# Filler matmuls that end with the first FFN tile, a wider planned pipe, and the first batch's mixing ahead

## Chip, cores and metric

The kernel runs on one core of a Trainium2 chip. The metric is the device time of one execution in microseconds. Before the change the median of three runs is 1138.97 us (1134.53 to 1140.03 us).

## What is computed

The inputs are q, k and v of 8 batches, 8 heads, 576 positions and 64 columns a head, all float32, and two FFN weights.

1. Attention with a mask. Heads 0 to 3 see the last 32 positions, heads 4 to 7 every fourth of the last 128. Scores are scaled by 1/8; softmax; product with v.
2. The heads are laid side by side: x of 8 batches, 576 rows, 512 columns.
3. Mixing: `u = x + real(fft(fft(x, axis=rows), axis=columns))`, then `un`, which is u with mean 0 and variance 1 per row.
4. FFN: `u + relu(un @ w_ch1) @ w_ch2`, hidden width 2048.

## The kernel before, in words

Every instruction is added to a plan (class `Plan`) with its engine, a cost in us, the buffers that it reads and writes, and a priority, lower first. `Plan.run` is a list scheduler: it plays the operations through with these costs, gives each free engine the ready operation with the lowest priority, and so fixes the order of the instructions on each engine, TensorE, VectorE, ScalarE, POOL and SP's DMA queue among them. Only the order goes to the chip; there every engine keeps it and waits where data is late. Planned times are used for nothing else, so an operation that carries an earliest time (`at`) doesn't wait for it on the chip.

The plan knows one pipe for all transfers: each takes the pipe for its bytes divided by 2.7e5 (bytes per us, line 322) and is done 1.6 us later. At most eight transfers of an issuing engine are open at a time. Buffers of a kind form a ring: a buffer is placed in the order of creation, and only when the one that had its slot is finished with.

The work has two halves. In the first, three kinds run side by side on TensorE:

- attention: per batch twelve steps, each with score matmuls (line 546), the mask with a minimum on VectorE (555), the exponential on ScalarE (561), transposes (574) and their copy (577), the product with v (581) and the scaling (593). Step u of batch b has priority 12b + u. A batch needs four loads each of `tq`, `kb` and `vt`; there are two `tq`, three `kb` and four `vt` buffers. Results go to DRAM (628) with priority plus `P_ST`, or `P_ST0` for batch 0.
- mixing, per batch: loads (700, 709), folds on POOL and VectorE (712 to 736), matmuls with cosine and sine tables along rows (763, 785) and columns (809, 815), sums on POOL (677, 679), normalisation (642 to 656). Its priority is 12(b + 1) + `P_MIX` + `P_SPAN` * x with x from 0 to 1; batches 0 and 1 have `P_MIX0`, `P_SPAN0` and `P_MIX1`, `P_SPAN1`. Its loads add `P_FD`, for batch 0 `P_FD0`. The tables `seq`, `tail`, `chn` and `alt` are loaded through POOL's queue with `at` from `T_SEQ` and `T_CHN`.
- the early FFN: the first 6 of 16 hidden blocks for each pair of 128-row tiles. `fill` writes up matmuls (943), a ReLU split in a high and a low part (949, 951), and down matmuls (959). It has priority `P_FILL` + `P_FILLT` * tile, 45 and up. The up results and the sums of the down matmuls take turns on two PSUM banks, the ring `ff`.

Weights come as float64 and are converted and split on the chip: `prep_w(f, ...)`, for f from 0 to 5, loads two blocks of 512 KB (881) into stage buffers of the ring `ut` (four slots) and runs one ScalarE, four VectorE, one ScalarE and one POOL operation on each (882 to 901); the POOL operation in line 901 is the last and is called the split below. The priority is `P_W` + `P_WF` * f, that of the load is `P_WD` lower. The same ring `ut` gives the operand buffer of each early-FFN pair (669, 670), created after the twelve stages.

In the second half, from the last line-959 matmul on, the other ten hidden blocks are done by lines 1204 and 1240 for all rows in nine equal chunks.

The zero fillers (line 492) are matmuls on a tile of zeros whose result nobody reads. There are `NSPIN` = 150 groups of two, with priority 900, so the plan puts one in wherever TensorE would have nothing else to do, group n from 0.4n us on. Their target is one tile of the ring `ff`, the first that is created.

Of the kernel before, what the change touches and what calls it, by code (L numbers as in the profile page):

```python
# [32 lines left out]
NH = 8  # L33
NXB = 6
NLATE = 4
NSPIN = 150
NPE = 1
LO1 = 'DVE'
NFA = 5
P_QK0, P_V0 = -8.0, -7.0  # L40
P_ST, P_FD, P_WD, P_ST0, P_FD0, P_SPAN0, P_SPAN1 = -4.0, -12.0, -10.0, 0.0, 0.0, 8.0, 13.0
P_QK, P_V, P_TR, P_MIX, P_SPAN, P_W, P_WF, P_FILL, P_FILLT = -8.0, -7.0, -5.0, 2.0, 13.0, 8.0, 8.0, 45.0, 4.0
P_MIX0, P_MIX1 = 3.0, 0.0
T_SEQ, T_CHN = 16.0, 24.0
NCH = B * S // TOK
NREST = 4 * B
QB = 96
# [132 lines left out]
class Plan:  # L180
# [21 lines left out]
    def add(self, eng, cost, fn, r=(), w=(), prio=0.0, nbytes=0, at=0.0):  # L202
        op = Op()
        op.eng, op.cost, op.fn, op.prio, op.nbytes = eng, cost, fn, prio, nbytes
        op.num, op.after, op.ready, op.start = len(self.ops), [], at, None
        self.ops.append(op)
        deps, bufs = set(), {}
        for items, writes in ((r, False), (w, True)):
            for it in items:
                b, key = it if isinstance(it, tuple) else (it, None)  # L210
                bufs[id(b)] = b
                keys = set(b.writer) | set(b.readers) if key is None else {key, None}
                for x in keys:
                    if x in b.writer:
                        deps.add(b.writer[x])
                    if writes:
                        deps.update(b.readers.get(x, ()))
        for items, writes in ((r, False), (w, True)):
            for it in items:
                b, key = it if isinstance(it, tuple) else (it, None)  # L220
                if writes:
                    if key is None:
                        b.writer, b.readers = {None: op.num}, {}
                    else:
                        b.writer[key] = op.num
                        b.readers.pop(key, None)
                else:
                    b.readers.setdefault(key, []).append(op.num)
        op.bufs = list(bufs.values())
        for b in op.bufs:  # L230
            b.left += 1
        deps.discard(op.num)
        op.waits = len(deps)
        for d in deps:
            self.ops[d].after.append(op)
        return op

    def run(self):
        ops = self.ops
        busy = {}  # L240
        avail, soon = {}, {}
        turn = {t: 0 for t in self.tags}
        events = [0.0]
        dma = 0.0
        for o in ops:
            busy.setdefault(o.eng, 0.0)
            avail.setdefault(o.eng, [])
            soon.setdefault(o.eng, [])
            if not o.waits:
                heapq.heappush(soon[o.eng], (o.ready, o.num))  # L250
                heapq.heappush(events, o.ready)
        order = []
        used, clock = {}, [0, False]
        lanes = {e: [] for e in busy}

        def place(o, now):
            need = []
            if o.nbytes and len(lanes[o.eng]) >= 8 and lanes[o.eng][-8] > now:
                return False
            for b in o.bufs:  # L260
                if b.tag is None or b.ap is not None or b.free_at is not None:
                    continue
                line, k = self.tags[b.tag], turn[b.tag]
                if line[k] is not b:
                    return False
                if k == 0 and any(x.left or x.free_at > now for t in self.behind.get(b.tag, ()) for x in self.tags.get(t, ())):
                    return False
                if k >= self.slots[b.tag]:
                    old = line[k - self.slots[b.tag]]
                    if old.left or old.free_at > now:  # L270
                        return False
                need.append(b)
            for b in need:
                turn[b.tag] += 1
                b.free_at = -1.0
            return True

        while events:
            now = heapq.heappop(events)
            while events and events[0] <= now:  # L280
                heapq.heappop(events)
            again = True
            while again:
                again = False
                for eng in busy:
                    if busy[eng] > now:
                        continue
                    while soon[eng] and soon[eng][0][0] <= now:
                        _, n = heapq.heappop(soon[eng])
                        heapq.heappush(avail[eng], (ops[n].prio, n))  # L290
                    held, got = [], None
                    while avail[eng]:
                        e = heapq.heappop(avail[eng])
                        if place(ops[e[1]], now):
                            got = ops[e[1]]
                            break
                        held.append(e)
                        if len(held) > 60:
                            break
                    for e in held:  # L300
                        heapq.heappush(avail[eng], e)
                    if got is None:
                        continue
                    again = True
                    got.start = now
                    order.append(got)
                    cost = got.cost
                    if eng == "PE":
                        win = int(now / WINDOW)
                        while clock[0] < win:  # L310
                            load = used.get(clock[0], 0.0) / WINDOW
                            clock[1] = load > 0.45 if clock[1] else load > 0.75
                            clock[0] += 1
                        cost *= 1 if clock[1] else 2
                        used[win] = used.get(win, 0.0) + min(cost, (win + 1) * WINDOW - now)
                        used[win + 1] = used.get(win + 1, 0.0) + max(0.0, now + cost - (win + 1) * WINDOW)
                    end = now + cost
                    busy[eng] = end
                    heapq.heappush(events, end)
                    done = end  # L320
                    if got.nbytes:
                        dma = max(dma, end + 0.9) + got.nbytes / 2.7e5
                        done = dma + 1.6
                        lanes[eng].append(done)
                        heapq.heappush(events, done)
                    for a in got.after:
                        lag = self.OWN[eng] if a.eng == eng else self.LAG[eng]
                        a.ready = max(a.ready, done + lag)
                        a.waits -= 1
                        if not a.waits:  # L330
                            heapq.heappush(soon[a.eng], (a.ready, a.num))
                            heapq.heappush(events, a.ready)
                    for b in got.bufs:
                        b.left -= 1
                        b.free_at = max(b.free_at or 0.0, done + self.LAG[eng])
                        if not b.left:
                            heapq.heappush(events, b.free_at)
        if len(order) != len(ops):
            left = [o for o in ops if o.start is None]
            raise RuntimeError(f"{len(left)} operations can't be placed: {[(o.eng, o.num, o.prio) for o in left[:5]]}")  # L340
        self.length = max(busy.values())
        for o in order:
            o.fn()
# [20 lines left out]


SOON = -1.0
WINDOW = 4096 / 1200
PLAIN_MASK = (1, 0, 0, 0, 0, 0)
DIL_MASK = (1, 2, 0, 1, 2, 0)
# [3 lines left out]
def fused_kernel(ctx: ExitStack, tc, q, k, v, w1, w2, seq, tail, chn, alt, mask, ident, perm, flip, out):  # L373
    nc = tc.nc
    plan = Plan()
    add = plan.add
# [43 lines left out]
    def bank(tag):  # L420
        return ring(tag, views[tag])
# [53 lines left out]
    def start():  # L475
# [9 lines left out]
        for n, t in enumerate(kbs):  # L485
            zero(t, "DVE", 0.1, lambda t=t: nc.vector.memset(t()[:, 0:WIN], 0.0), "z", -6.0 + n)
        zero(blank, "DVE", 0.3, lambda: nc.vector.memset(blank().bitcast(F32), 0.0), None, -9.0)
        spin = bank("ff")
        for n in range(NSPIN):
            def turn_over():  # L490
                for _ in range(2):
                    nc.tensor.matmul(spin()[:, :2 * P], lhsT=blank()[:, :P], rhs=blank()[:, P:3 * P], start=True, stop=True)  # L492
            add("PE", 0.22, turn_over, (blank,), (spin,), 900.0, at=0.4 * n)
        for t in xs + xtail:
            zero(t, "DVE", 0.07, lambda t=t: nc.vector.memset(t()[:, C:C + 1], 0.0), "pad")
        def gaps():
# [825 lines left out]
```

## Time and profile before

| what | value |
|---|---|
| median of three runs | 1138.97 us |
| profiled execution, its own time | 1143.46 us |
| span in the profile | 1141.7 us |
| TensorE busy | 1097.8 us (96%) |
| VectorE busy | 737.1 us (65%) |
| ScalarE, POOL busy | 520.6 us (46%), 516.2 us (45%) |
| granted TensorE clock, mean | 0.987 |
| zero fillers, busy | 45.6 us in 300 matmuls, from 1.4 to 115.1 us |

The profile is that of one execution. Busy shares are means over stages with different limits, and matmuls of 492 count as busy like all others. PE is TensorE, DVE is VectorE, ACT is ScalarE, SPq is SyncE's DMA queue. PEclk 1.00 is 2.4 GHz; a value between 0.5 and 1 is a mix in time of 2.4 and 1.2 GHz.

### The profile page before, as it was taken

What the parts mean: (1) busy time and instruction counts of PE and PEld (TensorE: products, weight loads), DVE (VectorE), ACT (ScalarE), POOL (GpSimd) and SP (SyncE); (2) the same over time, 40 slices, a digit from 0 to 9 for tenths busy, and PEclk for the clock granted to TensorE, in tenths of its full rate; (3) what the DMA queues carried; (4) which work ended last, traced back from release to release, by engine and by line L of the source; (5) the groups of instructions that cost most, each with busy time, mean ns of one, the idle gap of its engine ahead of it and who ended that gap; (6) DMA issues with size and microseconds to landing.
All of it is one profiled execution on the core that took longest, in us unless ns stands there. A gap on an engine that the chain in (4) does not pass through costs nothing.

```text
span 1141.7 us, 21571 instructions
## 1 busy us (share of the span) xinstructions
PE 1097.8 (96%) x7750; PEld 976.1 (85%) x7750; DVE 737.1 (65%) x2177; ACT 520.6 (46%) x1282; POOL 516.2 (45%) x636
## 2 busy tenths in 40 slices
PE   9999999999999999999999999999999999999996
PEld 8887877897888888798988889898989898988885
DVE  6578978776576667877674437382837465555636
ACT  5566655465455353433442434334343434343432
POOL 2134553642253225463321466455564637372834
PEclk9998999999989999999999999999999999999998
DMA  9665646745373424344354303231415041423121
GB/s 329 182 219 174 193 133 182 216 144 168 113 207 95 141 75 132 130 139 134 103 161 102 120 1 80 78 93 57 110 39 139 19 130 38 111 58 91 56 75 38
DMA packets 103804, 137.14 MB, mean 120 GB/s; under 512 B 9144, under 2 KB 61816, under 8 KB 103696
## 3 DMA queue, kind: packets, MB, share of 16 engines
q1 hardware_dynamic: 100128, 126.85, 37.5%
q0 software_dynamic: 3040, 8.09, 2.4%
q8 instruction: 61, 1.00, 0.4%
q10 hardware_dynamic: 528, 0.82, 0.2%
q14 instruction: 47, 0.39, 0.1%
HBM read 97.92 MB, written 37.80 MB: 119 GB/s over the span
## 4 chain that ended last, share of the span: by engine, by line
PE 74%; DVE 13%; ACT 4%; issue 3%; POOL 2%; DMA 2%; SPq 0%; DVEq 0%; POOLq 0%; ACTq 0%
PE bank L1204 21%; PE bank L1240 17%; PE bank L943 10%; PE bank L959 9%; PE bank L581 4%; PE bank L546 4%; PE bank L809 2%; PE bank L574 2%; DVE low L901 2%; DVE pm L555 2%; PE bank L763 2%; PE bank L492 2%; ACT low L1083 2%; ACT pm L561 1%; DMA tq<-in_q_dram 1%
## 5 line engine op out<-in xcount | busy, mean ns | idle before, releaser
L1204 PE MATMUL bank<-low,wb 128*128 128x512 f32 x1080 | 264.9, 394 | 0.0
L1204 PEld LDWEIGHTS bank<-low,wb 128*128 128x128 f32 x1080 | 196.4, 188 | 41.8 <-POOL low L1086 3.5
L943 PE MATMUL bank<-ut,low 128*128 128x256 f32 x1296 | 176.5, 289 | 4.3 <-DVE low L951 3.2
L943 PEld LDWEIGHTS bank<-ut,low 128*128 128x128 f32 x1296 | 163.7, 193 | 8.0 <-DVE low L951 5.0
L561 ACT ACTIVATE pm<-pm,mx 96x128 f32<-96x128 f32 x384 | 131.5, 394 | 63.0 <-DVE mx L555 60.8
L1240 PEld LDWEIGHTS bank<-w2s,low 128*128 128x128 f32 x1134 | 144.9, 189 | 12.8 <-DVE low L901 6.7
L959 PE MATMUL bank<-low 128*128 128x512 f32 x648 | 155.0, 392 | 0.5 <-DVE low L951 0.5
L1240 PE MATMUL bank<-w2s,low 128*128 128x256 f32 x1134 | 150.1, 282 | 5.2 <-DVE low L901 4.7
L959 PEld LDWEIGHTS bank<-low 128*128 128x128 f32 x648 | 119.1, 188 | 24.1 <-DVE low L951 0.7
L901 DVE TENSOR_TENSOR low<-y,low 128x640 fp32r<-128x640 f32 x90 | 83.4, 927 | 86.3 <-ACT low L899 86.3
L899 ACT CAST low<-y 128x640 fp32r<-128x640 f32 x90 | 65.6, 729 | 153.1 <-POOL y L1226 118.8
L555 DVE CUSTOM_DVE_ANT_0 pm<-bank,mask_sb 96x128 f32<-96x128 f32 x384 | 92.6, 279 | 38.7 <-PE bank L546 37.1
L1222 POOL TENSOR_TENSOR y<-xa 128x256 f32<-128x256 f32 x45 | 33.3, 740 | 180.9 <-ACT xa L1210 180.8
L901 DVE TENSOR_TENSOR low<-xa,low 128x256 fp32r<-128x256 f32 x45 | 33.4, 743 | 119.6 <-ACT low L899 119.6
L1240 PE MATMUL bank<-low 128*128 128x256 f32 x756 | 98.7, 284 | 2.4 <-DVE low L901 2.3
L1240 PEld LDWEIGHTS bank<-low 128*128 128x128 f32 x756 | 94.7, 191 | 7.2 <-DVE low L901 5.0
L1210 ACT ACTIVATE xa<-bank 128x256 f32<-128x256 f32 x90 | 34.5, 384 | 129.4 <-PE bank L1204 128.3
L581 PE MATMUL bank<-vt,ptsb 128*96 128x65 f32 x768 | 85.7, 252 | 4.9 <-DVE xt L593 4.9
L581 PEld LDWEIGHTS bank<-vt,ptsb 128*96 128x96 f32 x768 | 78.0, 168 | 13.0 <-DVE xt L593 7.4
L951 DVE SCALAR_TENSOR_TENSOR low<-bank,low 128x256 fp32r<-128x256 f32 x108 | 45.3, 421 | 62.9 <-ACT low L949 62.2
L1033 DVE TENSOR_TENSOR ut<-ut,bank 128x512 f32<-128x512 f32 (+1 forms) x144 | 75.3, 548 | 4.6 <-PE bank L1240 1.3
L1066 DVE STREAM_TRANSPOSE ut<-ut 128x512 f32<-128x512 f32 (+1 forms) x76 | 70.8, 977 | 11.2 <-DMA ut<-us 11.1
(129 smaller groups left out, 1767.3 us busy)
## 6 DMA issues: line engine op xcount, KB each, us to landing
vt<-in_v_dram SPq DMA_DIRECT2D x32, 390.0 KB
wst<-in_w_dram SPq DMA_DIRECT2D x20, 512.0 KB
us<-uc SPq DMA_DIRECT2D x36, 257.0 KB
tq<-in_q_dram SPq DMA_DIRECT2D x32, 288.0 KB
part<-row SPq DMA_DIRECT2D x36, 256.0 KB
ut<-us SPq DMA_DIRECT2D x36, 256.0 KB
ut<-part SPq DMA_DIRECT2D x36, 256.0 KB
kb<-in_k_dram SPq DMA_DIRECT2D x31, 288.0 KB
```

Of the source, the lines that this page charges most:

```text
L546: nc.tensor.matmul(sc()[e][:QB, KB * n:KB * n + KB], lhsT=tq()[ps, QB * t:QB * t + QB], rhs=kb()[ps, QB * t:QB * t + KB], start=True, stop ...
L555: nc.vector.tensor_tensor_reduce(pm()[:, i], sc()[i % 2][:QB, KB * (i // 2):KB * (i // 2) + KB], mask_sb()[:, masks[blocks[i // 2]]], -0.1 ...
L561: add("ACT", 0.295, lambda i=i: nc.scalar.activation(out=pm()[:, i], in_=pm()[:, i], func=AF.Exp, bias=mx()[:, i:i + 1], scale=-1.0), ((mx ...
L581: add("PE", 0.16, lambda i=i: nc.tensor.matmul(av()[:QB, 65 * i:65 * i + 65], lhsT=pt()[:, i], rhs=vt()[:, i % 2, blocks[i // 2]], start=T ...
L899: add("ACT", act(n), lambda: nc.scalar.copy(out=dst(0), in_=src()), need, ((key[0], (key[1], 0)),), prio)
L901: add(eng, (pool if eng == "POOL" else dve)(n), lambda: lo.tensor_tensor(out=dst(1), in0=src(), in1=dst(0).bitcast(F32), op=ALU.subtract), ...
L943: nc.tensor.matmul(z()[:, :n_tok], lhsT=wf()[:, a, kk], rhs=ut()[:, p, kk], start=(kk == 0 and n == 0), stop=(kk == KT - 1 and n == 2),)
L959: nc.tensor.matmul(acc(), lhsT=h()[:, a, P * s:P * s + P], rhs=wf()[:, p], start=(first and n == 0), stop=(last and n == 2),)
L1033: add("DVE", dve(C if at in (outer, inner) else TOK1), lambda: nc.vector.tensor_tensor(out=blocks(part())[:, at], in0=blocks(part())[:, at ...
L1066: nc.vector.transpose(out=o[back], in_=x[:, g])
L1204: nc.tensor.matmul(z(), lhsT=wb1[NF1 + 2 * p + f]()[:, a, kk], rhs=ut()[:, x, kk], start=(kk == 0 and n == 0), stop=(kk == KT - 1 and n == 2),
L1240: nc.tensor.matmul(acc()[block // 2][:, TOK1 * (block % 2):TOK1 * (block % 2) + TOK1], lhsT=hl()[:, a, i], rhs=w2s[p]()[:, j, x], start=(o ...
```

## The change

Four things are changed in the plan; the instructions of the computation are the same, and only their order can differ.

- The filler's target is a fixed PSUM bank, no longer a member of the ring `ff`. There are 250 groups, and once the plan has placed the first buffer of `ff`, a filler costs nothing and issues nothing.
- The plan's pipe carries 3.6e5 bytes per us for transfers that are issued in its first 40 us, and 2.7e5 from then on.
- For batch 0, stores and fold loads get an offset of -14 (was 0), mixing an offset of -14 (was 3) and a span of 4 (was 8).
- The early weights get priority 24 + 4f (was 8 + 8f); the tables' earliest planned times are 20 and 27 us (were 16 and 24).

```diff
--- before.py
+++ after.py
@@ -33,15 +33,15 @@
 NH = 8
 NXB = 6
 NLATE = 4
-NSPIN = 150
+NSPIN = 250
 NPE = 1
 LO1 = 'DVE'
 NFA = 5
 P_QK0, P_V0 = -8.0, -7.0
-P_ST, P_FD, P_WD, P_ST0, P_FD0, P_SPAN0, P_SPAN1 = -4.0, -12.0, -10.0, 0.0, 0.0, 8.0, 13.0
-P_QK, P_V, P_TR, P_MIX, P_SPAN, P_W, P_WF, P_FILL, P_FILLT = -8.0, -7.0, -5.0, 2.0, 13.0, 8.0, 8.0, 45.0, 4.0
-P_MIX0, P_MIX1 = 3.0, 0.0
-T_SEQ, T_CHN = 16.0, 24.0
+P_ST, P_FD, P_WD, P_ST0, P_FD0, P_SPAN0, P_SPAN1 = -4.0, -12.0, -10.0, -14.0, -14.0, 4.0, 13.0
+P_QK, P_V, P_TR, P_MIX, P_SPAN, P_W, P_WF, P_FILL, P_FILLT = -8.0, -7.0, -5.0, 2.0, 13.0, 24.0, 4.0, 45.0, 4.0
+P_MIX0, P_MIX1 = -14.0, 0.0
+T_SEQ, T_CHN = 20.0, 27.0
 NCH = B * S // TOK
 NREST = 4 * B
 QB = 96
@@ -255,6 +255,8 @@
 
         def place(o, now):
             need = []
+            if o.prio == SPIN and turn["ff"]:
+                o.cost, o.fn = 0.0, lambda: None
             if o.nbytes and len(lanes[o.eng]) >= 8 and lanes[o.eng][-8] > now:
                 return False
             for b in o.bufs:
@@ -319,7 +321,7 @@
                     heapq.heappush(events, end)
                     done = end
                     if got.nbytes:
-                        dma = max(dma, end + 0.9) + got.nbytes / 2.7e5
+                        dma = max(dma, end + 0.9) + got.nbytes / (PIPE0 if end < T_PIPE else PIPE1)
                         done = dma + 1.6
                         lanes[eng].append(done)
                         heapq.heappush(events, done)
@@ -364,6 +366,8 @@
 
 
 SOON = -1.0
+SPIN = 900.0
+PIPE0, PIPE1, T_PIPE = 3.6e5, 2.7e5, 40.0
 WINDOW = 4096 / 1200
 PLAIN_MASK = (1, 0, 0, 0, 0, 0)
 DIL_MASK = (1, 2, 0, 1, 2, 0)
@@ -485,12 +489,12 @@
         for n, t in enumerate(kbs):
             zero(t, "DVE", 0.1, lambda t=t: nc.vector.memset(t()[:, 0:WIN], 0.0), "z", -6.0 + n)
         zero(blank, "DVE", 0.3, lambda: nc.vector.memset(blank().bitcast(F32), 0.0), None, -9.0)
-        spin = bank("ff")
+        spin = Buf(ap=zs[0])
         for n in range(NSPIN):
             def turn_over():
                 for _ in range(2):
                     nc.tensor.matmul(spin()[:, :2 * P], lhsT=blank()[:, :P], rhs=blank()[:, P:3 * P], start=True, stop=True)
-            add("PE", 0.22, turn_over, (blank,), (spin,), 900.0, at=0.4 * n)
+            add("PE", 0.22, turn_over, (blank,), (spin,), SPIN, at=0.4 * n)
         for t in xs + xtail:
             zero(t, "DVE", 0.07, lambda t=t: nc.vector.memset(t()[:, C:C + 1], 0.0), "pad")
         def gaps():
```

## Rows read from the trace of the kernel before

**Rows 1.** Windows: length, busy of PE, PEld, DVE, ACT, POOL, PEclk, DMA share, GB/s.

```profile
0.00:48.10 48.10, 44.74 (x406) 41.32 (x406) 28.39 (x154) 25.65 (x69) 10.80 (x18) 1.00 0.87 284
48.10:85.00 36.90, 34.21 (x338) 30.79 (x338) 27.97 (x145) 24.58 (x69) 10.59 (x13) 1.00 0.60 188
85.00:118.70 33.70, 31.09 (x264) 26.74 (x262) 27.92 (x128) 21.92 (x60) 17.75 (x23) 0.90 0.55 180
118.70:200.00 81.30, 74.22 (x632) 64.59 (x632) 68.38 (x306) 48.64 (x136) 37.31 (x48) 0.98 0.58 168
200.00:643.00 443.00, 431.17 (x3152) 384.63 (x3150) 303.44 (x1042) 203.81 (x514) 166.40 (x209) 0.98 0.46 136
643.00:1141.70 498.70, 482.37 (x2971) 428.03 (x2969) 281.05 (x404) 196.03 (x437) 273.38 (x328) 0.99 0.26 74
```

**Rows 2.** Source view, lines 943, 959, 1204: durations, first and last start in us.

```profile
L943 PE MATMUL bank<-ut,low x1296: 274/281/581, 118.7 to 634.7; 128*128 128x256 f32 x186
...
L959 PE MATMUL bank<-low x648: 387/389/501, 158.2 to 642.8; 128*128 128x512 f32 x162
...
L1204 PE MATMUL bank<-low,wb x1080: 387/393/501, 643.0 to 1111.0; 128*128 128x512 f32 x180
```

**Rows 3.** Windows, instructions of line 492 alone (the zero fillers).

```profile
0.00:48.10 48.10, 27.06 (x180) 24.31 (x180) 1.00 0.87 284
85.00:118.70 33.70, 4.05 (x22) 3.54 (x22) 0.90 0.55 180
```

**Rows 4.** Chain of waits to 48.1 us and from there to 85 us.

```profile
by line: PE bank L492 30.5%; DMA tq<-in_q_dram 20.6%; PE bank L581 12.3%; PE bank L546 11.0%; PE bank L574 5.6%; DVE pm L555 5.1%; ACT pm L561 3.3%; issue 1.9%; SPq L532 1.2%; SPq L530 0.9%; SPq L476 0.9%; SPq L478 0.9%; SPq L477 0.9%; DVE 
...
3.69 9.90 DMA tq<-in_q_dram
...
37.09 4.10 PE bank L492 x34
...
by line: PE bank L492 18.0%; PE bank L546 16.1%; PE bank L581 15.0%; DMA vt<-in_v_dram 12.9%; DVE pm L555 11.9%; ACT pm L561 6.1%; PE bank L574 6.0%; DVE xt L593 4.4%; issue 2.3%; ACT ptsb L577 2.0%; SPq L532 1.2%; SPq L530 1.2%; SPq L531 1
```

**Rows 5.** Timeline of VectorE near 42 us: start, us, instruction, idle before it.

```profile
41.88 0.16 DVE L589 TENSOR_SCALAR sums<-bank 96x4 f32<-96x4 f32 x1 [5.23 <-PE bank L581]
```

**Rows 6.** Waits of SP's queue, 0 to 60 us: total, times, longest.

```profile
SPq L532 <- PE bank L581: 9.1, 1, 9.1
SPq L628 <- DVE mx L555: 8.3, 4, 3.4
```

**Rows 7.** Windows of the DMA-bound stretch and of the hole behind it.

```profile
10.00:20.00 10.00, 8.91 (x94) 8.00 (x93) 6.89 (x47) 7.49 (x24) 0.00 (x0) 1.00 1.07 391
20.00:30.00 10.00, 9.81 (x94) 8.81 (x92) 8.84 (x39) 6.13 (x15) 5.26 (x7) 1.00 0.96 321
36.50:49.00 12.50, 12.50 (x123) 12.40 (x121) 4.61 (x14) 3.55 (x9) 2.56 (x2) 1.00 0.50 162
```

**Rows 8.** Source view of line 901 on POOL to 160 us (the weight splits).

```profile
L901 POOL TENSOR_TENSOR low<-ut,low x12: 1258/1280/1743, 22.6 to 147.5; 128x512 fp32r<-128x512 f32 x12
```

**Rows 9.** Timelines of POOL and ScalarE around the ninth split.

```profile
105.69 1.27 POOL L901 TENSOR_TENSOR low<-ut,low 128x512 fp32r<-128x512 f32 x1 [1.28 <-ACT low L899]
...
108.21 0.58 ACT L669 CAST ut<-bank 128x512 fp32r<-128x512 f32 x1
```

**Rows 10.** DMA view, 0 to 36.5 us: queues, then issues with KB each.

```profile
q0 software_dynamic: 1440, 2.82, 27.0%
...
ut<-in_w_dram SPq DMA_DIRECT2D x6, 512.0 KB
...
seq<-in_seq_dram POOLq DMA_DIRECT2D x4, 290.0 KB, 8.0
...
tail_sb<-in_tail_dram POOLq DMA_DIRECT2D x1, 435.0 KB, 8.2
```

**Rows 11.** Windows, the stretch with the low clock.

```profile
104.00:116.00 12.00, 10.12 (x69) 8.41 (x68) 8.83 (x43) 5.64 (x15) 7.46 (x11) 0.72 0.38 127
```

**Rows 12.** Timeline of TensorE near 106 us.

```profile
106.28 0.63 PE L809 MATMUL bank<-chn,y 128*128 128x258 f32 x3 [1.39 <-DVE sq L825]
```

## The prediction

> **What bounds the kernel now.** I read the span by stages first [rows 1], because one busy share hides three different regimes. From 200 us on TensorE is busy for 431.2 of 443 us and then 482.4 of 498.7 us. At 643 us the last early-FFN matmul makes way for the late FFN without a pause [rows 2]. So the middle of the kernel always has early-FFN work in hand, and whatever TensorE loses before the first FFN tile is carried to the end: a microsecond of TensorE time won back early ends the kernel one microsecond sooner. The question is thus what TensorE loses early.
>
> The busy column is misleading there. TensorE looks busy for 44.7 of the first 48.1 us, yet 27.1 us of that are the zero fillers of line 492 [rows 3]. Are they harmless padding? The chain of waits says no: fillers are 30.5% of the chain in the first 48.1 us and 18.0% in the next 36.9 us [rows 4], that is 0.305 x 48.1 = 14.7 us and 0.180 x 36.9 = 6.6 us. The program order on TensorE is fixed by the list schedule, so a filler that the plan put into a wait runs even when the wait doesn't exist on the chip. The largest is a run of 34 fillers, 4.1 us at 37.1 us; VectorE stands idle 5.2 us behind it [rows 5], and a load of `vt` on SP's queue waits 9.1 us for the matmul that should free its buffer [rows 6]. In 36.5 to 49 us VectorE works 4.6 of 12.5 us and the DMA engines are half idle, after 391 and 321 GB/s in 10 to 30 us [rows 7]. Everything there waits for fillers. The reason is in the plan: it counts 2.7e5 bytes per us (270 GB/s) for transfers that in these rows went at 321 to 391 GB/s, so it expects data late and pads.
>
> **The change part by part.**
>
> The wider pipe. 3.6e5 for the plan's first 40 us lies between the two rates seen, so planned arrivals come close to the real ones and most padding before about 40 us has no planned wait to fill. Removable: between 0 and the whole 14.7 us. What is late next? The matmuls that the fillers held back then meet VectorE and ScalarE, each busy 25 to 28 us of these 48 [rows 1], which is room for a stage of some 36 us, and the pipe, which is full until 36 us. I take 10 us, two thirds, since some fillers cover real waits. For the 6.6 us of fillers on the chain in 48 to 85 us the plan's pipe is as narrow as before, if they lie past its 40 us; bounds 0 and 6.6 us, I take 2, for those the shifted stage brings inside.
>
> Filler count and bank. 250 instead of 150 costs nothing by itself, since fillers fill planned gaps only and now end when the plan places the first FFN tile. What is won there is at most the 22 fillers, 4.05 us busy, that run in 85 to 118.7 us [rows 3]. That the filler tile held one of two FFN banks cost nothing: the first FFN matmul starts at 118.7 us [rows 2], behind the last filler of that row's stretch, and the other bank was free for it.
>
> First batch's mixing ahead. Its ten stores go from priorities 0 to 11 down to -14 to -3, its eight loads from 15 to -16, its vector and matrix work from 15 to 23 down to -2 to 2: ahead of all of the second batch's attention (12 to 23). Work is moved, not removed. The stretch 85 to 118.7 us shows what it could win: 33.7 - 31.1 = 2.6 us idle, a granted clock of 0.90, so 0.10 x 33.7 = 3.4 us, and 22 x 0.12 = 2.7 us of fillers, at the pitch of that run of 34: 8.7 us [rows 1, 3, 4]. But the first FFN operand needs a `ut` buffer, and the twelve weight stages come before it in a ring of four, so it must wait for the ninth weight split. On the trace that split starts at 105.69 us and takes 1.28 us (median of all twelve), and the copy into the operand follows at 108.2 us [rows 8, 9]. The ninth split belongs to f=4, whose priority is 8 + 8 x 4 = 40 before and 24 + 4 x 4 = 40 after. So this gate stays; bounds 0 and 8.7 us, I take 2.
>
> Weights later. f=0 goes from priority 8 to 24, f=5 from 48 to 44. Each of six loads in the first 36.5 us is 512 KB [rows 10]; the first two, 1.05 MB, now come behind the `vt` loads of the first batch, which lands those 1.05 / 0.391 = 2.7 us sooner. That is inside the 14.7 us bound, not on top. Late splits threaten the first FFN tile only: its down matmuls start at 158.2 us, 40 us after its first up matmul, because the twelfth split starts at 147.5 us [rows 2, 8]. f=5 a little earlier is worth 0 to the 7.1 us that TensorE idles in 118.7 to 200 us [rows 1]; I take 0, since VectorE is busy 68 of these 81 us and sets the pace.
>
> Constants. POOL's queue carries 2.82 MB of tables [rows 10]. Only their order among POOL's instructions matters: today `seq` and `tail`, 4 x 290 + 435 KB = 1.63 MB, are issued at once and the rest, 1.19 MB, behind the first weight split at 22.6 us [rows 8]. If with weights late all go first, the first batch's loads come 1.19 / 0.391 = 3.0 us later; if `seq` goes behind the split too, 1.63 / 0.391 = 4.2 us sooner. I take 0, and both ends stay.
>
> SP's queue. Stores placed earlier make SP wait at them, with the next batch's loads behind: four such waits for VectorE cost SP 8.3 us, 3.4 at most [rows 6]. A loss of 0 to 3.4 us; I take 1.
>
> The rest, 200 to 643 us, is reshuffled by any change of order: TensorE idles 11.8 us there and the clock, 0.98, costs 0.02 x 443 = 8.9 us [rows 1]. A quarter of these 20.7 us either way, 5 us; I take 0.
>
> Sum: 10 + 2 + 2 - 1 = 13 us. Against the profiled execution, 1143.5 us with a span of 1141.7, that gives 1130.5 us. It lies 0.4% above the median of the runs, 1139.0 us, so the forecast for the median is 1139.0 - 13 = 1126 us.
>
> **The clock, weighed.** Between 104 and 116 us the granted clock is 0.72, a mix of the 1.2 and 2.4 GHz levels, though TensorE is busy 10.1 of 12 us [rows 11]; matmuls run slow behind a pause of 1.39 us at 106.3 us [rows 12]. The clock costs 0.28 x 12 = 3.4 us there. The Trainium skill (TensorE: Matmul & The Clock Gate, HAM oscillation) speaks against this change: bursts of matmuls with waits between them fall back to the slow clock, and each burst starts slow again, so after the first tile, with no fillers left, it would fall more often. By the row alone I book nothing for it, since in 118.7 to 200 us the clock is 0.98 with no fillers at all [rows 1]; by the rule the price is the fourth case below.
>
> **The rivals.**
>
> 1. Forecast: 6 to 20 us won, 1119 to 1133 us. Chance 0.50.
> 2. The padding goes entirely: 14.7 + 6.6 + 8.7 us and a part of the 7.1 us idle after the first tile, 20 to 33 us, 1106 to 1119 us. For it: the chip follows the plan's order closely, so better arrival times repair every step behind. Against it: real waits below the fillers, such as the 9.9 us on a load of `tq` that end at 13.6 us [rows 4]. Chance 0.20.
> 3. The gate doesn't move: VectorE's work up to the first tile, 28.4 + 28.0 + 27.9 = 84.3 us [rows 1], and the ninth split at priority 40 are as before, so the first tile comes at 115 us or later and the filler time comes back as idle time. With the 5 us of reshuffle the gain is -5 to 6 us, 1133 to 1144 us. Against it: VectorE has 118.7 - 84.3 = 34 us to spare. Chance 0.18.
> 4. Slower: after the first tile nothing fills TensorE's gaps, and the clock falls. If the tile starts 15 us sooner but the twelfth split stays at 147.5 us, the exposed stretch is 40 + 15 = 55 us; at 0.72 it loses 0.28 x 55 = 15 us. With 5 us of the gain kept, 1139 + 10 = 1149 us. It decides if the clock after the first tile stays below about 0.76 for 55 us, where the loss eats all 13 us. Against it: today's 0.98 without fillers. Chance 0.12.
>
> **How the numbers follow.** 0.5%, 5.7 us, is about what a measurement of this kernel can tell from no change. Faster by more (under 1133.3 us): cases 1 and 2, 0.70. Within it: 0.18. Slower: 0.12. The range reaches down to 1110 us, which leaves out the lowest third of case 2, and up to 1143 us, which leaves out most of case 4: about 0.07 and 0.11 outside. It holds the bounds of the constants (4.2 and 3.0 us) and of the reshuffle (5 us) around 1126.
>
> **What would show it.** The first FFN matmul before 112 us, last early-FFN matmul near 630 instead of 643 us, and the late stage its 498.7 us long as now. Filler time on the chain in the first 48 us under 5 us; the VectorE hole and the half-idle pipe at 36.5 to 49 us gone. Wrong: fillers on the chain as before (the pipe's width didn't reach the schedule), or a first tile near 118 us with idle TensorE ahead of it (case 3), or a granted clock under 0.8 behind the first tile (case 4).

## The result and the profile after

The median after the change is 1122.88 us (four runs, 1121.21 to 1124.06) against 1139.50 us before (four runs, 1134.53 to 1142.07). The ratio is 0.9858, with a 95% interval of 0.9829 to 0.9887: 16.6 us are won (the difference of the medians), where 13 were forecast (1126 us). The profiled execution after took 1124.05 us, with a span of 1122.3 us.

The change moves lines: 492 is 496 now, 581 is 585, 901 is 905, 943 is 947, 959 is 963, 1204 is 1208. The first FFN tile is here the first up result, the twelve up matmuls of one hidden block into one PSUM bank, and the second tile the next such result. The late stage is the second half, the late FFN.

First the windows of the changed kernel by the same stages as in [rows 1], cut at its own first FFN tile and at its own last early-FFN matmul, and the window that stood half empty in [rows 7]:

```profile
0.00:48.10 48.10, 42.90 (x400) 36.83 (x400) 34.57 (x207) 34.21 (x93) 12.90 (x18) 1.00 0.93 316
48.10:85.00 36.90, 33.29 (x313) 30.03 (x314) 30.31 (x135) 25.15 (x70) 14.02 (x16) 1.00 0.70 233
85.00:105.90 20.90, 18.94 (x170) 17.33 (x168) 18.24 (x82) 12.23 (x34) 13.55 (x17) 0.92 0.38 109
105.90:200.00 94.10, 89.85 (x789) 78.71 (x788) 81.22 (x380) 58.88 (x163) 49.88 (x66) 1.00 0.62 183
200.00:619.40 419.40, 411.68 (x3013) 368.37 (x3012) 278.65 (x966) 193.45 (x486) 145.75 (x184) 0.99 0.46 134
619.40:1122.30 502.90, 483.61 (x2971) 428.26 (x2969) 286.61 (x414) 197.98 (x440) 282.29 (x335) 1.00 0.27 75
36.50:49.00 12.50, 10.73 (x109) 8.53 (x106) 10.13 (x64) 9.55 (x29) 3.59 (x3) 1.00 0.77 277
```

Then the source view of the lines of [rows 2], and the fillers by window, as in [rows 3]:

```profile
L947 PE MATMUL bank<-ut,low x1296: 274/281/561, 105.9 to 611.1; 128*128 128x256 f32 x186
L963 PE MATMUL bank<-low x648: 387/389/481, 148.2 to 619.1; 128*128 128x512 f32 x162
L1208 PE MATMUL bank<-low,wb x1080: 387/393/502, 619.4 to 1091.4; 128*128 128x512 f32 x180
```

```profile
0.00:48.10 48.10, 17.48 (x96) 14.30 (x96) 1.00 0.93 316
48.10:85.00 36.90, 11.27 (x80) 9.99 (x80) 1.00 0.70 233
```

The hole at 36.5 us is gone. VectorE works 10.1 of the 12.5 us from 36.5 to 49 us, where it worked 4.6, and the DMA share is 0.77 instead of 0.50 [rows 7]. The first FFN tile starts at 105.9 us, 12.8 us sooner, and the last early-FFN matmul at 619.1 instead of 642.8 us, 23.7 us sooner [rows 2]. So nearly half of it, 10.9 us, is won behind the first tile: from 200 us to the end of the early FFN TensorE idles 419.4 - 411.7 = 7.7 us, before 11.8 [rows 1], and it is busy 19.5 us less (411.7 against 431.2), in part because of the clock (0.99 against 0.98). The late stage gives 4.2 us back, 502.9 instead of 498.7 us: 3.0 us more idle TensorE (19.3 against 16.3) and 1.2 more busy.

23.6 us at the end of the early FFN less those 4.2 make 19.4 us between the two spans, not 16.6: the profiled execution of before lay 4.0 us above the median of its four runs, that of the changed kernel 1.2 us.

Rows of the timelines of POOL, ScalarE and TensorE after the change (start, length) tell what became of the gate of the ninth weight split and of the first batch:

```profile
91.96 1.71 POOL L905 TENSOR_TENSOR low<-ut,low 128x512 fp32r<-128x512 f32 x1
```

```profile
97.21 0.59 ACT L673 CAST ut<-bank 128x512 fp32r<-128x512 f32 x1 [1.50 <-PE bank L666]
```

```profile
44.84 0.89 PE L585 MATMUL bank<-vt,ptsb 128*96 128x65 f32 x8 [0.40 <-DVE xt L597]
```

and of TensorE before:

```profile
52.46 0.89 PE L581 MATMUL bank<-vt,ptsb 128*96 128x65 f32 x8 [0.36 <-DVE xt L593]
```

The split starts at 91.96 instead of 105.69 us [rows 9], and the copy into the FFN operand then waits 1.50 us for transposes (line 666), not for the split's buffer. A step has eight matmuls of the product with v; the twelfth group of eight, that of the first batch's last step, starts at 44.84 us, before at 52.46, 7.6 us sooner.

### The profile page after: what moved, and what is told of

It reads as the page before. It is cut to its first block, busy times and chain, and to the rows that moved or that the text cites. A ratio compares the mean times of both kernels' runs of the same rounds, so it can differ in the third digit from the quotient of the medians.

```text
span 1122.3 us, 21365 instructions
## 1 busy us (share of the span) xinstructions
PE 1080.3 (96%) x7648; PEld 959.5 (85%) x7648; DVE 729.6 (65%) x2177; ACT 521.9 (47%) x1282; POOL 518.4 (46%) x636
## 4 chain that ended last, share of the span: by engine, by line
PE 77%; DVE 12%; POOL 4%; issue 3%; ACT 3%; DMA 1%; SPq 0%; DVEq 0%; POOLq 0%; ACTq 0%
PE bank L1208 19%; PE bank L1244 15%; PE bank L963 13%; PE bank L947 12%; PE bank L585 5%; PE bank L550 4%; DVE pm L559 3%; PE bank L813 3%; PE bank L578 2%; PE bank L767 2%; DVE low L905 2%; PE bank L496 1%; ACT low L1087 1%; POOL y L1230 1%; DVE ut L1037 1%
## 5 line engine op out<-in xcount | busy, mean ns | idle before, releaser
L947 PE MATMUL bank<-ut,low 128*128 128x256 f32 x1296 | 172.4, 287 | 0.1
L947 PEld LDWEIGHTS bank<-ut,low 128*128 128x128 f32 x1296 | 161.1, 190 | 2.5 <-DVE low L955 0.6
```

The costliest lines, as they stand in the source:

```text
L947: nc.tensor.matmul(z()[:, :n_tok], lhsT=wf()[:, a, kk], rhs=ut()[:, p, kk], start=(kk == 0 and n == 0), stop=(kk == KT - 1 and n == 2),)
```

## The experiments

Letters in the quoted expectations mark theories; a digit behind one marks a variant. A: the wider pipe wins by removing padding. B: the first batch's mixing sets the first tile. C: the gain is a better packing of the middle. D: the wider pipe pays only when the fillers no longer hold a bank of the ring. E: fillers hold the order back. F: the clock. G: fillers cover waits that are real. H: the late weights cause the 4 us lost at the end. I: the parts trade against each other.

All results in one table: the median, the ratio to before (run beside it) with its interval, and from each profile, in us, the start of the first up tile and of the last early down matmul, and the length of the late stage (span less start of its first matmul).

| kernel | median us | ratio | first tile | last down | late stage |
|---|---|---|---|---|---|
| e1_pipe: before + pipe | 1142.07 | 1.0044 [1.0026, 1.0061] | 112.1 | 639.1 | 498.8 |
| e2_fill: before + filler part | 1137.80 | 1.0001 [0.9982, 1.0019] | 117.6 | 636.1 | 498.6 |
| e3_mix: before + mixing ahead | 1133.85 | 0.9970 [0.9955, 0.9985] | 119.7 | 631.2 | 498.7 |
| e4_wts: before + weights, tables | 1141.63 | 1.0032 [1.0014, 1.0049] | 120.0 | 640.5 | 498.9 |
| p1_pipefill: before + pipe + filler part | 1122.92 | 0.9843 [0.9812, 0.9875] | 112.4 | 616.7 | 504.8 |
| p2_end: pipe, fillers in the ring but ended early | 1130.97 | 0.9937 [0.9916, 0.9958] | 116.6 | 633.3 | 498.9 |
| e5_nopipe: after, narrow pipe | 1133.98 | 0.9946 [0.9917, 0.9974] | 115.7 | 626.7 | 502.8 |
| e6_nowts: after, old weights, tables | 1129.47 | 0.9913 [0.9881, 0.9945] | 112.4 | 624.9 | 502.5 |
| e6b_nomix: after, old mixing | 1121.56 | 0.9827 [0.9794, 0.9861] | 112.6 | 618.8 | 502.3 |
| e7_bskip: before, almost no fillers | 1151.95 | 1.0109 [1.0056, 1.0162] | 131.9 | 653.4 | 498.8 |
| e8_askip: after, almost no fillers | 1137.31 | 0.9999 [0.9981, 1.0016] | 123.0 | 633.6 | 502.6 |
| x_late: after, late weights' priority | 1121.07 | 0.9863 [0.9832, 0.9893] | 105.8 | 617.6 | 501.5 |

The runs were made in four groups, each with before beside it: e1 to e4; p1, e5, e6 and e6b; e7 and e8; p2 and x_late. The medians of before were 1137.97, 1139.62, 1137.45 and 1137.58 us.

### Each part alone

**e1_pipe**

```diff
-                        dma = max(dma, end + 0.9) + got.nbytes / 2.7e5
+                        dma = max(dma, end + 0.9) + got.nbytes / (PIPE0 if end < T_PIPE else PIPE1)
...
+PIPE0, PIPE1, T_PIPE = 3.6e5, 2.7e5, 40.0
```

> The kernel before with the wider planned pipe alone (3.6e5 bytes per us for the plan's first 40 us). Theory A, the prediction's main term: padding on the chain of waits is what the narrow pipe put there, so this part alone wins 8 to 14 us (1126 to 1131 us), the fillers' share of the chain in the first 48 us falls from 30% under 15%, and the first FFN tile comes at 105 to 110 us. Theory B, the first batch's mixing sets the first tile: this part alone wins under 4 us, and the first tile stays at 114 us or later. Theory C, what is won is a better packing of the middle that any new order can bring: the first tile moves little, and the time changes by up to 10 us through idle time and clock behind 200 us.

**e2_fill**

```diff
-NSPIN = 150
+NSPIN = 250
...
+            if o.prio == SPIN and turn["ff"]:
+                o.cost, o.fn = 0.0, lambda: None
...
-        spin = bank("ff")
+        spin = Buf(ap=zs[0])
```

> The kernel before with the filler part alone (own bank, 250 groups, none after the first FFN tile is placed). Theories A and B: within 3 us of before, since only 4 us of fillers run in the 34 us ahead of the first tile and the bank is free for it. Rival, the clock: with no fillers behind the first planned tile the granted clock falls there, and the time is 3 to 15 us longer. Theory C: any time within 10 us of before, with the difference behind 200 us.

**e3_mix**

```diff
-P_ST, P_FD, P_WD, P_ST0, P_FD0, P_SPAN0, P_SPAN1 = -4.0, -12.0, -10.0, 0.0, 0.0, 8.0, 13.0
+P_ST, P_FD, P_WD, P_ST0, P_FD0, P_SPAN0, P_SPAN1 = -4.0, -12.0, -10.0, -14.0, -14.0, 4.0, 13.0
...
-P_MIX0, P_MIX1 = 3.0, 0.0
+P_MIX0, P_MIX1 = -14.0, 0.0
```

> The kernel before with the first batch's mixing ahead alone (offsets of -14, span 4). Theory A: 0 to 4 us won, because the operand buffer of the first FFN tile still waits for the ninth weight split, which keeps its priority 40; the first tile stays within 4 us of 118.7 us. Theory B: 8 us or more won, and the first tile at 108 us or earlier. Theory C: the difference lies behind 200 us.

**e4_wts**

```diff
-P_QK, P_V, P_TR, P_MIX, P_SPAN, P_W, P_WF, P_FILL, P_FILLT = -8.0, -7.0, -5.0, 2.0, 13.0, 8.0, 8.0, 45.0, 4.0
+P_QK, P_V, P_TR, P_MIX, P_SPAN, P_W, P_WF, P_FILL, P_FILLT = -8.0, -7.0, -5.0, 2.0, 13.0, 24.0, 4.0, 45.0, 4.0
...
-T_SEQ, T_CHN = 16.0, 24.0
+T_SEQ, T_CHN = 20.0, 27.0
```

> The kernel before with the later early weights and the later tables alone. Theory A: within 4 us of before; the ninth split keeps its priority, so the first tile stays within 5 us of 118.7 us. Rival: with the first weights out of the way the first batch's attention ends several us sooner, and 5 us or more are won. Theory C: the difference lies behind 200 us.

Measured: no part alone makes the gain. The pipe, on which the forecast put 10 of its 13 us, loses 4.1 us by the medians (ratio 1.0044). The filler part gives nothing, the mixing wins 4.1 us, the weights cost 3.7. Added up that is a loss of some 3.5 us, where the whole change wins 16.6. For e1_pipe theory A fails (8 to 14 us and a first tile by 110 us were expected); e2_fill and e4_wts came out as theory A had it, and e3_mix at the upper end of it; its 4 us sit behind the first tile, which came at 119.7 us, as theory C had it.

The pipe alone does close the hole: from 36.5 to 49 us VectorE then works 10.8 of 12.5 us. It also brings the first tile forward, 112.1 instead of 118.7 us. So why does it lose? Its TensorE timeline shows it:

```profile
112.11 1.58 PE L944 MATMUL bank<-ut,low 128*128 128x256 f32 x12
113.53 1.11 PE L493 MATMUL bank<-blank 128*128 128x256 f32 x8
...
156.32 0.48 PE L493 MATMUL bank<-blank 128*128 128x256 f32 x2
156.64 0.51 PE L944 MATMUL bank<-ut,low 128*128 128x256 f32 x3
```

Twelve up matmuls run, then none for 43 us, and the thirteenth comes straight behind the very last filler. The filler tile is a member of the ring `ff`, whose two banks take up results and down sums in turn, and a bank is passed on only when everything written to it is done. In the order of before that is harmless, since all 300 filler matmuls are spent by 115.1 us, ahead of the first tile. The wider pipe leaves fewer waits to fill, so 76 filler matmuls still run behind 112 us, and the second FFN tile must wait until the last of them has found a gap.

### Parts together, and parts taken out

**p1_pipefill**: the edits of e1_pipe and e2_fill.

> The kernel before with the wider planned pipe and the filler part together (own bank, 250 groups, none after the first FFN tile). The trace of the pipe alone shows one up tile of the early FFN at 112.1 us and the next at 156.6 us, straight behind the last filler at 156.3 us. Theory D: with the wider pipe the 150 groups last longer than the way to the first tile, so they hold one of the two FFN banks for 44 us; with both parts that block is gone, the up tiles follow one another from about 112 us, and 8 to 12 us are won against before (1126 to 1130 us). Rival, the pipe's order is itself no better: the time stays within 5 us of before though the block is gone, and the gain of the whole change needs the mixing ahead.

**e5_nopipe**

```diff
-PIPE0, PIPE1, T_PIPE = 3.6e5, 2.7e5, 40.0
+PIPE0, PIPE1, T_PIPE = 2.7e5, 2.7e5, 40.0
```

> The changed kernel with the plan's pipe at 2.7e5 throughout: filler part, mixing, weights and tables. Theory D: most of the gain goes, 1133 to 1140 us, and the fillers' share of the chain in the first 48 us is back near 30%. Rival, the gain is the mixing's and a bank's: 1128 us or less.

**e6_nowts**: the changed kernel with the old values of e4_wts.

> The changed kernel with the early weights and tables at their old priorities and times: pipe, filler part and mixing ahead. Theory D: the weights part alone lost 4 us, so without it the time is 1118 to 1125 us, not longer than the changed kernel's. Rival: with the mixing ahead the weights have to make room on VectorE, and without that the time is 1128 us or more.

**e6b_nomix**: the changed kernel with the old values of e3_mix.

> The changed kernel without the first batch's mixing ahead: pipe, filler part, weights and tables. Theory D: the mixing ahead is worth about what it won alone, 4 us, so 1125 to 1129 us. Rival, mixing and pipe need one another: 1132 us or more.

Measured: p1_pipefill takes 1122.92 us, the whole gain and 3 us more than theory D expected. Its timeline has no block, the second tile's nine matmuls follow the first's twelve at once:

```profile
112.39 2.64 PE L947 MATMUL bank<-ut,low 128*128 128x256 f32 x21
114.87 0.81 PE L585 MATMUL bank<-vt,ptsb 128*96 128x65 f32 x8
115.49 0.60 PE L947 MATMUL bank<-ut,low 128*128 128x256 f32 x3
```

The windows from 112 to 160 us, of the fillers and of the up matmuls alone (length, then busy time of PE and of PEld, PEclk, DMA share, GB/s), first of e1_pipe:

```profile
112.00:160.00 48.00, 13.40 (x76) 10.02 (x75) 1.00 0.56 164
112.00:160.00 48.00, 3.58 (x25) 3.24 (x26) 1.00 0.56 164
```

and of p1_pipefill:

```profile
112.00:160.00 48.00, 0.49 (x2) 0.30 (x2) 1.00 0.58 165
112.00:160.00 48.00, 10.93 (x72) 9.15 (x72) 1.00 0.58 165
```

Where e1_pipe runs 76 fillers, p1_pipefill runs 47 more up matmuls, 10.93 - 3.58 = 7.4 us of early FFN in gaps that zeros had filled. The windows from 200 us to the end of the early FFN, of e1_pipe and of p1_pipefill, give the whole:

```profile
200.00:639.30 439.30, 426.32 (x3130) 378.91 (x3130) 300.77 (x1023) 203.27 (x512) 157.76 (x197) 1.00 0.47 136
```

```profile
200.00:616.90 416.90, 409.82 (x3032) 367.64 (x3032) 280.46 (x979) 194.26 (x490) 150.19 (x190) 1.00 0.48 136
```

p1_pipefill has 426.3 - 409.8 = 16.5 us less TensorE work left at 200 us, and idles 7.1 us behind it where e1_pipe idles 13.0, a further 5.9. The late stage goes 6.0 us the other way (504.8 against 498.8). 16.5 + 5.9 - 6.0 = 16.4 us, all by which the two profiled executions differ (1139.88 and 1123.48 us).

The pipe's part is shown from the other side by e5_nopipe: without it the changed kernel takes 1133.98 us, 11.1 us more (10 by the two ratios), as theory D had it. The rest of the change adds nothing that can be told to p1_pipefill: 1122.88 against 1122.92 us. Inside it two effects cancel. With the mixing ahead but the old weights (e6_nowts) the time is 1129.47 us, 6.6 us worse (the rival's 1128 or more, not theory D's); with the weights changed but the old mixing (e6b_nomix) it is 1121.56 us, below both expectations and not to be told from the changed kernel. So the mixing that alone wins 4 us costs 6.6 on top of pipe and filler part, and the later weights, which alone cost 3.7, take that away again. Why they do isn't shown.

### How long the ring is held

**p2_end**: e1_pipe with the fillers still in the ring, but costing and issuing nothing once the first FFN tile has its bank. There are 250 groups, as in the changed kernel.

```diff
-NSPIN = 150
+NSPIN = 250
...
+            if o.prio == SPIN and turn["ff"] > 1:
+                o.cost, o.fn = 0.0, lambda: None
```

> The kernel before with the wider planned pipe, and fillers that keep their place in the FFN ring but end once the plan has placed the first FFN tile's bank. Theory D2: what matters is that fillers end; then the bank is free a moment later, the up tiles follow one another, and the time is that of pipe and own bank together, 1119 to 1127 us. Rival: the fixed bank matters by itself, and the second up tile still comes late; 1130 us or more.

Measured: 1130.97 us, between e1_pipe and p1_pipefill, and what the rival expected. Its last filler runs at 116.23 us, and yet the second tile comes 11.7 us behind the first:

```profile
116.23 0.49 PE L496 MATMUL bank<-blank 128*128 128x256 f32 x2
116.56 1.57 PE L947 MATMUL bank<-ut,low 128*128 128x256 f32 x12
...
128.24 0.60 PE L947 MATMUL bank<-ut,low 128*128 128x256 f32 x3
```

So the hold is the plan's and not the chip's: the emptied groups issue nothing, but they keep their priority 900 and their earliest planned time, 0.4n us, and the bank is passed on only when the last of the 250 is placed, which can't be before 0.4 x 249 = 99.6 us of the plan. That this makes the 11.7 us is argued from the code; no run with fewer groups shows it. So p2_end doesn't show that a place in the ring costs by itself, only what a shorter hold costs. With the same wider pipe, a second tile 44.5 us behind the first, 11.7 us behind, and at once goes with 1142.07, 1130.97 and 1122.92 us. In executions with a mean clock of 0.997 p2_end took 1130.81 and 1131.97 us, and p1_pipefill 1122.24 and 1122.39 us, so the clock doesn't make this difference.

The fixed bank isn't another bank, either. In the code `zs[0]` is one of the two banks of the ring `ff`; the fillers still write to it, but the plan no longer counts them as its users, and they end before the first tile needs it.

### Are the fillers themselves the cost?

**e7_bskip** is before and **e8_askip** the changed kernel, with every instruction where the plan put it, but with all filler groups behind the first fourteen left out, 272 of the 300 filler matmuls and 170 of the 198. Nobody reads the zeros that they would write.

```diff
-            def turn_over():
-                for _ in range(2):
+            def turn_over(n=n):
+                for _ in range(2 if n < 14 else 0):
```

> The kernel before with its plan and the order of everything else unchanged, but with filler groups 14 and up not issued (the plan still books their time). Theory E, fillers run where the chip has no wait and hold the order back: the 21 us of fillers on the chain up to 85 us shrink to the real waits, and 8 to 18 us are won (1121 to 1131 us) as long as the granted clock stays up. Rival F, the clock: with the gaps empty the granted clock falls to 0.7 or so in the first 100 us, matmuls take up to twice as long there, and the time is within 5 us of before or longer. Rival G, fillers cover real waits: the idle time takes their place one for one, and the time stays within 3 us of before with the clock up.

> The changed kernel with its plan and order unchanged, but with filler groups 14 and up not issued. Fillers are 11 us of its chain up to 48 us, 5 us of them ahead of the first attention step, and some 6 us from there to the first tile. Theory E: 4 to 9 us won (1114 to 1119 us). Rival F: the granted clock falls ahead of the first tile, and the time is 1123 us or more. Rival G: within 3 us of the changed kernel.

Measured: both lose, as rival F had it. e7_bskip takes 1151.95 - 1137.45 = 14.5 us more than before; e8_askip takes 1137.31 - 1122.88 = 14.4 us more than the changed kernel, which ran beside other executions of before (by the two ratios, 0.9999 and 0.9858, it is 16 us). Windows from 30 to 100 us of before, e7_bskip, the changed kernel and e8_askip, in this order:

```profile
30.00:100.00 70.00, 66.35 (x635) 60.37 (x636) 50.26 (x257) 46.29 (x131) 16.64 (x18) 1.00 0.62 198
```

```profile
30.00:100.00 70.00, 57.83 (x338) 48.08 (x336) 40.88 (x208) 36.51 (x101) 15.17 (x18) 0.50 0.56 172
```

```profile
30.00:100.00 70.00, 63.17 (x585) 56.43 (x585) 59.17 (x268) 48.09 (x131) 29.90 (x31) 0.98 0.70 230
```

```profile
30.00:100.00 70.00, 57.56 (x364) 46.99 (x363) 45.92 (x220) 41.38 (x110) 19.44 (x19) 0.55 0.63 208
```

The granted clock falls from 1.00 to 0.50 and from 0.98 to 0.55, that is from 2.4 GHz to all or nearly all of the time at 1.2 GHz, over these 70 us, and VectorE gets 9 to 13 us less done in them. The difference between the two orders stays: 1151.95 - 1137.31 = 14.6 us without fillers, 16.6 with them. Part of the 14.6 is clock, since e7_bskip was granted less of it; of the executions with the same mean clock, 1145.35 and 1135.18 us at 0.968, and 1149.49 and 1138.53 at 0.963, the two orders lie 10.2 and 11.0 us apart. So most of the gain sits in the order of the work, not in the filler microseconds saved, and the fillers pay for themselves by the clock.

### The 4 us given back

**x_late**

```diff
-    FILL, LAST = 1000.0, 2000.0
+    FILL, LAST = 60.0, 2000.0
```

> The changed kernel with the late weights' priority at 60 + f instead of 1000 + f. In its trace the late stage lasts 502.9 us against 498.7 before, and its first late weight load is issued at 485 us against 453 before. Theory H: the late weights come too late for the first chunk, and earlier ones give the 4 us back: the late stage under 500 us and 1117 to 1121 us in all. Rival I, a trade: the weights' vector work then delays the early FFN's, which ends as much later, and the time stays within 2 us of the changed kernel or is longer.

Measured: inconclusive. The edit was to bring the late weights' loads forward, and hardly did: the first starts at 482.7 us, in the changed kernel at 485.0. The late stage is 501.5 us long and the time, 1121.07 us, is that of the changed kernel. What the table does show is that the stage has two lengths, 498.6 to 498.9 us in before, e1 to e4, p2 and e7, and 501.5 to 504.8 us in the others. They go with SP's waits at the late weight loads for the conversion that VectorE ends (line 901 before, 902 to 905 in the others): 4.4 to 4.5 us in all kernels of the first group, 7.6 to 8.9 us in all of the second. Two plans of the late weights, then. The end of the early FFN on the chip doesn't sort them: e3_mix ends it at 631.2 us and has the short stage, e8_askip at 633.6 us and has the long one. What picks the plan stays open.

## Why the prediction came out near, and where it was wrong

**Right.** What TensorE wins early is carried to the end of the early FFN: its last matmul came at 619.1 us, where near 630 was forecast, and before at 642.8. But the date of the first tile isn't the measure of it: p1_pipefill has its first tile 6.5 us later than the changed kernel (112.4 against 105.9) and ends its early FFN 2.4 us sooner (616.7 against 619.1). The pipe is needed: the hole at 36.5 us and the half-idle DMA are gone with it, and without it 11.1 us are lost. The first tile comes before 112 us. Case 4 is refuted: from 105.9 to 200 us the clock is 1.00 with no filler in it. Case 3's gate did move, by 13.7 us. Case 2, over 20 us, didn't come.

**Wrong: "That the filler tile held one of two FFN banks cost nothing".** This is the step that failed most. It was read from the trace of before, where it is true (e2_fill: 1.0001). But it is a statement about the order of before, where the fillers run out ahead of the first tile, and another part of the same change alters that order. Beside the wider pipe the filler part is worth some 20 us: it decides whether the pipe wins 16.7 us or loses 4.1, each against before run beside it.

**Wrong in kind: 10 us for the pipe, as a term of its own, taken from the fillers on the chain.** The terms don't add. What the pipe does alone in the stage from which the 10 us were taken is smaller, too: the first batch's last product with v starts at 49.9 us in e1_pipe and 49.8 in p1_pipefill, 2.6 to 2.7 us sooner than before. The price of a filler was also read from the wrong view: in the changed kernel they are still 22.8% of the chain in the first 48.1 us, 11.0 us, where under 5 were to be seen, and the row is this:

```profile
by line: PE bank L496 22.8%; PE bank L550 20.9%; DVE pm L559 15.2%; PE bank L585 13.3%; PE bank L578 9.1%; issue 4.2%; DVE xt L597 3.8%; DVE ut L897 2.1%; DVE ut L888 1.5%; DVE ut L894 1.2%; DVE rinv L596 1.1%; DVE blank L491 1.0%; ACT ptsb
```

In e5_nopipe, 11 us slower, it is 24.7% (near 30% was expected), so the share hardly follows the time. Being on the chain doesn't make them removable. Leaving them out cost 14.5 us (e7_bskip), with the granted clock down at 0.50. The reading that should have led is that of the order: what the plan puts behind a wait that it wrongly expects. With the wider pipe alone (e1_pipe) VectorE works 59.4 instead of 50.3 us between 30 and 100 us, and POOL 27.7 instead of 16.6; in the changed kernel it is 59.2 and 29.9. That this head start is what the middle of the kernel lives on is argued, not shown line by line.

**The rule on the clock.** What the rows show: 0.50 over 70 us as soon as the fillers are out ahead of the first tile, and 1.00 behind that tile without them. The Trainium skill (TensorE: Matmul & The Clock Gate, HAM oscillation) says that bursts of matmuls with waits between them fall back to the slow clock. Ahead of the first tile the runs agree with it, for either order: without the fillers TensorE waits there up to 3.6 us in e7_bskip and 5.7 in e8_askip. Behind it, where the forecast gave it 0.12 as case 4, the clock didn't fall: in the changed kernel TensorE is busy 89.9 of 94.1 us there, so the waits that the rule speaks of hardly came.

**Mis-sized.** Mixing ahead: 2 forecast; 4.1 alone, and a loss of 1.3 on top of all other parts (1122.88 against 1121.56), which the intervals don't tell from nothing. Weights and tables: 0 forecast and 0 in sum with the mixing, but as a loss of 3.7 alone and a gain of 6.6 in company. The 2 us for the fillers on the chain in 48 to 85 us, and SP's queue, 1: no run separates them; the fillers' share of that chain fell from 18.0 to 7.3%. (The first batch's ten stores had priorities 3 to 11, not 0 to 11; nothing hangs on it.) 200 us to the end of the early FFN: 0 forecast with 5 either way; the idle time fell by 4.1 us (11.8 to 7.7), and the clock there, 0.98 before and 0.99 after, cost 0.02 x 443 = 8.9 and 0.01 x 419 = 4.2 us. The clock's share belongs to the one execution and not to the kernel: e1_pipe and e2_fill, no faster than before, were granted 1.00 there.

**Not foreseen.** The late stage's 4.2 us, taken as unchanged. 16.6 instead of 13 thus is no confirmation of the sum: its largest term works only with a term booked at nothing, its sign flips without it, two parts booked at 2 and 0 turn out at minus 6.6 and plus 6.6 beside the others, and a loss that wasn't in it hides part of the gain.

## What to carry to other kernels

In a list schedule a filler isn't free just because it yields to everything: whatever it holds, here a bank of a ring, is held until the last of them has been placed, so fillers belong on a target for which the plan lets nobody wait, and must end before its first real user. Whether such a hold hurts can't be read from the trace of before when another edit of the same change alters the order; ask of each "costs nothing" which of the other edits could make it false, and run the parts in pairs as well as singly. Before filler time on the chain is booked as removable, look at what the granted clock does without it.

## What the runs showed of the hardware

TensorE's clock stayed at its lower level in stretches where the engine was busy nearly all the time. Two windows of e7_bskip, 10 us each:

```profile
50.00:60.00 10.00, 9.57 (x63) 7.88 (x62) 4.78 (x33) 4.68 (x14) 0.92 (x1) 0.50 0.31 85
...
110.00:120.00 10.00, 8.10 (x79) 7.10 (x78) 9.74 (x26) 6.30 (x16) 5.57 (x5) 1.00 0.59 178
```

In the first it is busy 9.57 us and the clock is 0.50, in the second busy 8.10 us at 1.00. The busy column alone doesn't tell the clock.

The same order of instructions was granted different clocks in two executions. p2_end and p1_pipefill have the same TensorE order up to the first FFN tile; from 60 to 70 us the first was granted 0.65 and the second 1.00, and its first FFN tile came 4.2 us later (116.6 against 112.4):

```profile
60.00:70.00 10.00, 10.00 (x73) 9.05 (x72) 5.39 (x27) 4.97 (x14) 3.96 (x4) 0.65 0.66 212
```

```profile
60.00:70.00 10.00, 9.35 (x92) 8.29 (x92) 8.69 (x44) 6.93 (x19) 3.35 (x3) 1.00 0.64 210
```

The times of one kernel spread with the clock, too. Of the 58 executions of before that ran beside the experiments the shortest took 1134.66 us at a mean clock of 0.998 and the longest 1144.94 us at 0.986. At a mean clock of 0.997 one of before took 1134.97 us and one of the changed kernel 1121.21 us, 13.8 us apart: some 3 of the 16.6 us may be that before was granted a little less clock in its four runs; only the clock of its profiled execution, 0.987, is on record.
